# Six small gaps in SBUF: moving a fused convolution-and-MLP kernel's weights and activations apart by 64 to 384 bytes

## The chip, the cores and the metric

The kernel runs on one core of one Trainium2 chip. The metric is the device time of one execution in microseconds (us); lower is better. A core has five engines that run side by side: TensorE (PE, the matrix engine, whose weight loads are shown apart as PEld), VectorE (DVE), ScalarE (ACT), GpSimd (POOL) and SyncE (SP, which here only issues transfers). They work on SBUF, a memory of 128 partitions; an array takes the same byte range in each partition, and the addresses below are byte addresses within a partition. TensorE writes into PSUM.

## The reference

```python
# x, v: (2, 12480, 128)   pos_emb: (12480, 64)
u = x * v
h = (relu(pos_emb @ w1) @ w2) * exp(-0.01 * pos)
y = irfft(rfft(u, 2S) * rfft(h, 2S))[:, :S]        # causal convolution along the sequence, per channel
t = (x * y).reshape(24960, 128)
hid = t @ w_in                                     # (24960, 2048)
g = maximum(0.01 * hid, hid)
out = g @ w_out                                    # (24960, 128)
```

All of it is float32 (the two MLP weights arrive as float64).

## The kernel before

The convolution is a two-stage Fourier transform of 98 x 128 points, done with matmuls against tables. It is computed for sequence 0 first, then for sequence 1 while the MLP of sequence 0 runs. The MLP takes the tokens in 50 tiles of at most 512 columns (46 of 512, two of 352, one of 390, one of 314). Its 2048 hidden channels are taken in 16 slices `f` of 128. Each float32 operand is split into a high and a low part of the type float32r (`zh` and `zl` for the tokens, `w_in_h` and `w_in_l`, and so on), and a product is three matmuls: high by high, high by low, low by high.

So one slice of one tile is six matmuls, and TensorE's stream is this group of six, 800 times over. `m1(k, f)` issues the first three, `m2` the second three for the slice three places earlier (`DEEP = 3`):

```python
nc.tensor.matmul(hp, w_in_h[:, fs], zh, start=True, stop=False)                 # L855
nc.tensor.matmul(hp, w_in_h[:, fs], zl, start=False, stop=False)                # L856
nc.tensor.matmul(hp, w_in_l[:, fs], zh, start=False, stop=True)                 # L857
...
nc.tensor.matmul(ap, w_out_h[:, f, :], rh, start=(f == 0 and at0[k] >= S), stop=False)   # L887
nc.tensor.matmul(ap, w_out_h[:, f, :], rl, start=False, stop=False)             # L888
nc.tensor.matmul(ap, w_out_l[:, f, :], rh, start=False, stop=(f == NF - 1))     # L889
```

The first operand is the one that is loaded into the array (128 columns, PEld, one load for each matmul), the second is streamed through it (the token tile). Between the two threes, ScalarE writes `rh` from `hp` and VectorE writes `rl`. For the 25 tiles of sequence 0, three more matmuls with `wc_h` and `wc_l` (L883 to L885) stand in front of slice 0. Between groups stand the matmuls that bring tokens in and out (`yp` L828, `zp` L836, `op` L911) and those of sequence 1's convolution (`cv` L408 in its first half, `cv` L137, also in threes and mostly of 512 columns, in its second).

The order of all instructions is written out by hand; no scheduler changes it. Arrays are laid out in SBUF in the order in which their pools and tiles are made: the weights stand in the pool `const`, near the start, in the order `ident`, `mb`, `w_in_h`, `w_in_l`, `w_out_h`, `w_out_l`, `wc_h`, `wc_l`; the streamed tiles stand in the pool `sm`, far behind: `zt` (padded to 856 floats, of which 512 are used), `zf`, `zh` and `zl` (three buffers each), `rh` and `rl` (five each). A slice `f` lies 512 bytes behind the slice before it, and a buffer 2048 bytes behind the one before it.

Of the kernel before, what the change touches and what calls it, by code (L numbers as in the profile page):

```python
# [8 lines left out]
F32 = mybir.dt.float32  # L9
# [21 lines left out]
def tile_conv_mlp(ctx, tc, x, v, pos_emb, w1, w2, w_in, w_out, cf, cr, cg, cb, ci, cw, out):  # L31
    nc = tc.nc
    B, S, D = x.shape
# [10 lines left out]
    const = ctx.enter_context(tc.tile_pool(name="const", bufs=1))  # L44
# [9 lines left out]

    ident = const.tile([128, 128], F32, name="ident")
    mb = const.tile([128, 2, 2, 64], F32, name="mb")
    w_in_h = const.tile([128, DFF], F32R, name="w_in_h")
    w_in_l = const.tile([128, DFF], F32R, name="w_in_l")
    w_out_h = const.tile([128, NF, D], F32R, name="w_out_h")
    w_out_l = const.tile([128, NF, D], F32R, name="w_out_l")  # L60
    wc_h = const.tile([128, D], F32R, name="wc_h")
    wc_l = const.tile([128, D], F32R, name="wc_l")
# [91 lines left out]
    def back(dp, parts, c):  # L154

        for s in range(2):
            for j, w in halves(c):
                three(dp[s][:, w], (mi_h[j][:, s], mi_l[j][:, s]), (parts[0][:, s, w], parts[1][:, s, w]))

    def turned(pool, psum, m2, m1):  # L160

        ph = pool.tile([128, 2, 2], F32, tag="ph0", name="ph0", bufs=1)
# [46 lines left out]
    with tc.manual_schedule():  # L209
# [22 lines left out]
        with ExitStack() as st:  # L232
# [81 lines left out]
            for c in range(NC0):  # L314
# [51 lines left out]
                for mm in range(MC):  # L366
                    a = psa.tile([NA, 2, 512], F32, tag="a", name="a", bufs=3)
# [430 lines left out]
        sm = ctx.enter_context(tc.tile_pool(name="sm", bufs=2, reuse_waits="tile"))  # L798
# [16 lines left out]
        def pieces_of(t):  # L815

            for k in range(NTL):
                lo, hi = max(at0[k], t * TOK), min(at0[k + 1], t * TOK + TOK)
                if lo < hi:
                    yield k, lo - at0[k], lo - t * TOK, hi - lo  # L820

        def front(t):

            cp, g, xt = ld.pop(t)
            yp = ps.tile([128, 4, D], F32, tag="io", name="yp")
            for q in range(4):
                for w in range(2):
                    nc.tensor.matmul(yp[64 * w:64 * w + 64, q, :], g[:NA, NA * q + w:NA * q + w + 127:2],  # L828
                                     cp[:, q // 2, w, q % 2, :], start=True, stop=True)
            zt = sm.tile([128, 856], F32, tag="zt", name="zt", bufs=1)[:, :4 * D].rearrange("a (q d) -> a q d", d=D)  # L830
            nc.vector.tensor_tensor(out=zt[:GAP], in0=yp[:GAP], in1=xt[:GAP].rearrange("a p m d -> a (p m) d"),
                                    op=ALU.mult)
            yield
            zp = ps.tile([128, 4, 128], F32, tag="io", name="zp")
            for q in range(4):
                nc.tensor.transpose(zp[:, q, :GAP], zt[:GAP, q, :], ident[:GAP, :GAP])  # L836
            zf = sm.tile([128, TOK], F32, tag="zf", name="zf", bufs=1)
            for w in range(2):
                nc.scalar.copy(zf[:, :2 * NA - 2].rearrange("d (m a) -> d m a", m=2)[:, :, w::2],
                               zp[:, 2:4, 64 * w:64 * w + KH - w])  # L840
            nc.scalar.copy(zf[:, 2 * NA - 2:].rearrange("d (m i w) -> d m w i", m=2, w=2),
                           zp[:, 0:2].rearrange("d m (w i) -> d m w i", w=2)[:, :, :, :KH])
            for k, a, c, n in pieces_of(t):
                if k not in z:
                    z[k] = [sm.tile([128, WIDE], F32R, tag=g, name=g, bufs=ZB) for g in ("zh", "zl")]
                zh, zl = (i[:, a:a + n] for i in z[k])
                nc.scalar.copy(zh, zf[:, c:c + n])  # L847
                (nc.gpsimd if t else nc.vector).tensor_tensor(out=zl, in0=zf[:, c:c + n], in1=zh, op=ALU.subtract)  # L848

        def m1(k, f):  # L850
            w = widths[k]
            zh, zl = (i[:, :w] for i in z[k])
            hp = ps.tile([128, WIDE], F32, tag="mh", name="mh", bufs=3)[:, :w]
            fs = slice(f * 128, f * 128 + 128)
            nc.tensor.matmul(hp, w_in_h[:, fs], zh, start=True, stop=False)  # L855
            nc.tensor.matmul(hp, w_in_h[:, fs], zl, start=False, stop=False)  # L856
            nc.tensor.matmul(hp, w_in_l[:, fs], zh, start=False, stop=True)  # L857
            rh = sm.tile([128, WIDE], F32R, tag="rh", name="rh", bufs=DEEP + 2)[:, :w]
            rl = sm.tile([128, WIDE], F32R, tag="rl", name="rl", bufs=DEEP + 2)[:, :w]
            if at0[k] < S:  # L860
                nc.scalar.activation(out=rh, in_=hp, func=AF.Relu)  # L861
                nc.vector.scalar_tensor_tensor(out=rl, in0=hp, scalar=0.0, in1=rh, op0=ALU.max, op1=ALU.subtract)  # L862
            else:
                tag, pool, bufs = (("s1", s0, 3), ("hd", psc["pool"], 2), ("ct1", psc["pool"], 1),
                                   ("s1", s0, 3), ("hd", psc["pool"], 2))[f % 5]
                r = pool.tile([128, 2048 if tag == "hd" else 1024], F32, tag=tag, name="r", bufs=bufs)[:, :w]
                nc.scalar.activation(out=r, in_=hp, func=AF.Lrelu, alpha=0.01)  # L867
                if f % 2:
                    nc.vector.tensor_copy(rh, r)  # L869
                else:  # L870
                    nc.scalar.copy(rh, r)  # L871
                nc.vector.tensor_tensor(out=rl, in0=r, in1=rh, op=ALU.subtract)  # L872
            return rh, rl
# [71 lines left out]
        def do(what, t):  # L945
            if what == "mult":
                mult_a(t)
            elif what == "conv":
                run(conv)
                load_tile(t)  # L950
                load_tile(t + 1)
            elif what == "load":
                if t not in ld:
                    load_tile(t)
            elif what == "join":
                join_hi(t)
                join_lo(t)
            elif t in fronts:
                next(fronts.pop(t), None)
            else:  # L960
                fronts[t] = front(t)
                next(fronts[t])

        SLOTS = ends[NT] - 14
        done = AHEAD
        frt = front(0)
        join_hi(0)
        join_lo(0)
# [18 lines left out]
        for k in range(NTL):  # L987
            for f in range(NF):
                i = k * NF + f
                pend.append((k, f, m1(k, f)))  # L990
                if len(pend) > DEEP:
                    m2(*pend.pop(0))
                for s_ in steps.get(i, ()):
                    do(*s_)
                if f == DEEP - 1 and k:
                    fin = finish(k - 1)
                if f >= DEEP - 1 and (f - DEEP + 1) % 2 == 0:
                    next(fin, None)
                if i < SLOTS:
                    while done < min(pieces, pace(i)):  # L1000
                        next(conv, None)
                        done += 1
# [71 lines left out]
```

## Time and profile before

| | |
|---|---|
| time, median of 3 runs | 1732.74 us (1730.29 to 1736.19) |
| the profiled execution's own time | 1735.8 us |
| its span from first to last instruction | 1734.0 us |
| TensorE busy | 1650.2 us, 95% of the span |
| VectorE, ScalarE, GpSimd busy | 64%, 57%, 48% |
| mean granted TensorE clock | 0.979 of full speed |
| MLP stage, from about 390 us to the end | 1344 us, TensorE busy 1325.75 us of it, clock 1.00 |

The profiled execution lies 3.1 us above the median, inside the spread of the runs. A matmul's row in the trace gives its start and the length of its record. The records of neighbours overlap, since matmuls are pipelined; what a matmul costs in a dense stretch is the step from its start to the next one's start, not the length of its record.

### The profile page before, as it was taken

To read this page: it belongs to the slowest core of one execution; us is meant where nothing else is said; L and a number is where in the kernel's file an instruction comes from. 1 tells how busy PE (TensorE), PEld (TensorE's weight loads), DVE (VectorE), ACT (ScalarE), POOL (GpSimd) and SP (SyncE) were. 2 spreads that over 40 slices of the span, in tenths; PEclk is the share of its full clock that TensorE was granted. 3 is DMA by queue.
4 is the path that set the end of the run, shared out by engine and by line. 5 is a ranking of instruction groups with operands and counts; after the bars stand their busy time and mean duration, and the time that the engine had idled before them with its cause. 6 is when DMAs were issued, how large, how long until landed. Compare 5 with 4: busy or idle time off the path is not lost.

```text
span 1734.0 us, 27418 instructions
## 1 busy us (share of the span) xinstructions
PE 1650.2 (95%) x9185; PEld 1327.1 (77%) x9185; DVE 1108.7 (64%) x1705; ACT 985.4 (57%) x2005; POOL 833.0 (48%) x858
## 2 busy tenths in 40 slices
PE   6788799889999999999999999999999999999998
PEld 5777455478888887877788777877787878787878
DVE  3586588744554565555555554577777777777775
ACT  1222354434444466666667666566666666666666
POOL 3444122243444277777768675343644454345430
PEclk9889899989999999999999999999999999999999
DMA  8898899964665475556565551222212122111200
GB/s 225 247 263 242 281 322 331 306 201 148 206 182 175 120 200 160 167 154 194 149 175 167 157 150 64 77 67 62 65 43 81 44 70 70 60 53 56 73 18 20
DMA packets 166679, 253.27 MB, mean 146 GB/s; under 512 B 14622, under 2 KB 119346, under 8 KB 163466
## 3 DMA queue, kind: packets, MB, share of 16 engines
q1 hardware_dynamic: 146378, 225.81, 44.8%
q10 hardware_dynamic: 20160, 25.70, 4.3%
q8 instruction: 73, 1.20, 0.3%
q14 instruction: 68, 0.56, 0.1%
HBM read 167.95 MB, written 83.43 MB: 145 GB/s over the span
## 4 chain that ended last, share of the span: by engine, by line
PE 78%; DMA 9%; DVE 5%; issue 3%; SPq 2%; ACT 2%; POOL 1%; ACTq 0%; POOLq 0%; DVEq 0%
PE mh L855 11%; PE mh L857 10%; PE mh L856 10%; PE acc L889 10%; PE acc L887 10%; PE acc L888 10%; PE cv L137 4%; PE yp L828 4%; PE cv L408 3%; DMA ft<-in_cf_dram 2%; DMA xt<-in_x_dram 2%; PE op L911 2%; DMA scr<-o 1%; PE zp L836 1%; DMA scr<-ct 1%
## 5 line engine op out<-in xcount | busy, mean ns | idle before, releaser
L862 DVE SCALAR_TENSOR_TENSOR rl<-mh,rh 128x512 fp32r<-128x512 f32 (+2 forms) x400 | 270.1, 677 | 311.3 <-ACT rh L861 306.9
L872 DVE TENSOR_TENSOR rl<-r,rh 128x512 fp32r<-128x512 f32 (+1 forms) x400 | 329.5, 837 | 113.3 <-ACT rh L871 105.7
L861 ACT ACTIVATE rh<-mh 128x512 fp32r<-128x512 f32 (+2 forms) x400 | 235.2, 590 | 211.7 <-PE mh L857 197.3
L867 ACT ACTIVATE r<-mh 128x512 f32<-128x512 f32 (+1 forms) x400 | 235.7, 590 | 184.8 <-PE mh L857 168.0
L855 PE MATMUL mh<-zh,w_in_h 128*128 128x512 f32 (+3 forms) x800 | 329.8, 412 | 1.9 <-ACT zh L847 1.3
L857 PE MATMUL mh<-zh,w_in_l 128*128 128x512 f32 (+3 forms) x800 | 310.5, 388 | 0.0
L887 PE MATMUL acc<-rh,w_out_h 128*128 128x512 f32 (+3 forms) x800 | 310.3, 388 | 0.0
L856 PE MATMUL mh<-zl,w_in_h 128*128 128x512 f32 (+3 forms) x800 | 310.0, 388 | 0.0
L889 PE MATMUL acc<-rh,w_out_l 128*128 128x512 f32 (+3 forms) x800 | 310.0, 388 | 0.0
L888 PE MATMUL acc<-rl,w_out_h 128*128 128x512 f32 (+3 forms) x800 | 308.3, 385 | 0.0
L848 POOL TENSOR_TENSOR zl<-zf,zh 128x390 fp32r<-128x390 f32 (+24 forms) x110 | 75.7, 702 | 349.7 <-ACT zh L847 349.5
L618 POOL TENSOR_TENSOR cp<-cq,cp 98x256 f32<-98x256 f32 x252 | 212.4, 843 | 19.8
L607 POOL TENSOR_TENSOR cp<-cin 98x256 f32<-98x256 f32 x126 | 104.5, 850 | 162.8 <-PE yp L828 118.7
L855 PEld LDWEIGHTS mh<-zh,w_in_h 128*128 128x128 f32 x800 | 151.1, 189 | 37.0 <-issue 9.9
L857 PEld LDWEIGHTS mh<-zh,w_in_l 128*128 128x128 f32 x800 | 150.8, 189 | 32.1
L888 PEld LDWEIGHTS acc<-rl,w_out_h 128*128 128x128 f32 x800 | 150.4, 188 | 32.1 <-DVE rl L872 0.6
L889 PEld LDWEIGHTS acc<-rh,w_out_l 128*128 128x128 f32 x800 | 150.3, 188 | 31.5
L887 PEld LDWEIGHTS acc<-rh,w_out_h 128*128 128x128 f32 x800 | 150.4, 188 | 30.4
L856 PEld LDWEIGHTS mh<-zl,w_in_h 128*128 128x128 f32 x800 | 151.5, 189 | 24.5 <-POOL zl L848 0.7
L869 DVE CAST rh<-r 128x512 fp32r<-128x512 f32 (+1 forms) x200 | 114.3, 572 | 38.4 <-ACT r L867 35.8
L871 ACT CAST rh<-r 128x512 fp32r<-128x512 f32 (+1 forms) x200 | 122.1, 611 | 6.4
L616 POOL TENSOR_TENSOR cq<-cin 98x256 f32<-98x256 f32 x126 | 113.3, 899 | 1.0 <-DMA cin<-scr 1.0
(154 smaller groups left out, 2359.0 us busy)
## 6 DMA issues: line engine op xcount, KB each, us to landing
cin<-scr SPq DMA_DIRECT2D x318, 98.0 KB
hd<-hspec SPq DMA_DIRECT2D x48, 512.0 KB
scr<-o SPq DMA_DIRECT2D x32, 588.0 KB
bin<-scr SPq DMA_DIRECT2D x23, 768.0 KB
scr1b<-o SPq DMA_DIRECT2D x32, 392.0 KB
hspec<-hs ACTq DMA_DIRECT2D x48, 256.0 KB
scr<-ct ACTq DMA_DIRECT2D x24, 512.0 KB
xm<-in_x_dram SPq DMA_DIRECT2D x128, 96.0 KB
```

The lines of the kernel that those rows point to most:

```text
L618: eng.tensor_tensor(out=cp[:, p, w], in0=cq[:, p], in1=cp[:, p, 1], op=op)
L855: nc.tensor.matmul(hp, w_in_h[:, fs], zh, start=True, stop=False)
L856: nc.tensor.matmul(hp, w_in_h[:, fs], zl, start=False, stop=False)
L857: nc.tensor.matmul(hp, w_in_l[:, fs], zh, start=False, stop=True)
L861: nc.scalar.activation(out=rh, in_=hp, func=AF.Relu)
L862: nc.vector.scalar_tensor_tensor(out=rl, in0=hp, scalar=0.0, in1=rh, op0=ALU.max, op1=ALU.subtract)
L867: nc.scalar.activation(out=r, in_=hp, func=AF.Lrelu, alpha=0.01)
L871: nc.scalar.copy(rh, r)
L872: nc.vector.tensor_tensor(out=rl, in0=r, in1=rh, op=ALU.subtract)
L887: nc.tensor.matmul(ap, w_out_h[:, f, :], rh, start=(f == 0 and at0[k] >= S), stop=False)
L888: nc.tensor.matmul(ap, w_out_h[:, f, :], rl, start=False, stop=False)
L889: nc.tensor.matmul(ap, w_out_l[:, f, :], rh, start=False, stop=(f == NF - 1))
```

## The change

Four tiles that nothing reads are put into `const`, one ahead of each of the MLP's four weight arrays (64, 256, 384 and 64 bytes); `zt`'s padding shrinks by 256 bytes; and a tile of 320 bytes that nothing reads is put ahead of `rh`. The line numbers in the diff are those of the kernel before.

```diff
@@ -54,9 +54,13 @@
     mb = const.tile([128, 2, 2, 64], F32, name="mb")
+    const.tile([128, 16], F32, name="gap_w_in_h")
     w_in_h = const.tile([128, DFF], F32R, name="w_in_h")
+    const.tile([128, 64], F32, name="gap_w_in_l")
     w_in_l = const.tile([128, DFF], F32R, name="w_in_l")
+    const.tile([128, 96], F32, name="gap_w_out_h")
     w_out_h = const.tile([128, NF, D], F32R, name="w_out_h")
+    const.tile([128, 16], F32, name="gap_w_out_l")
     w_out_l = const.tile([128, NF, D], F32R, name="w_out_l")
@@ -827,7 +831,7 @@
-            zt = sm.tile([128, 856], F32, tag="zt", name="zt", bufs=1)[:, :4 * D].rearrange("a (q d) -> a q d", d=D)
+            zt = sm.tile([128, 792], F32, tag="zt", name="zt", bufs=1)[:, :4 * D].rearrange("a (q d) -> a q d", d=D)
@@ -855,6 +859,8 @@
             nc.tensor.matmul(hp, w_in_l[:, fs], zh, start=False, stop=True)
+            if not k and not f:
+                sm.tile([128, 80], F32, tag="gap", name="gap", bufs=1)
             rh = sm.tile([128, WIDE], F32R, tag="rh", name="rh", bufs=DEEP + 2)[:, :w]
```

Every engine has the same instructions, in the same order, with the same waits, before and after; only addresses differ. The program places the arrays so (first buffer of each, bytes):

| array | before | after |
|---|---|---|
| `w_in_h` | 18048 | 18112 |
| `w_in_l` | 26240 | 26560 |
| `w_out_h` | 34432 | 35136 |
| `w_out_l` | 42624 | 43392 |
| `zh` | 149696 | 150208 |
| `zl` | 155840 | 156352 |
| `rh` | 161984 | 162816 |
| `rl` | 172224 | 173056 |

Everything else behind the gaps moves by 512 to 832 bytes, always by a multiple of 64. Since slices lie 512 bytes and buffers 2048 bytes apart, the distance from a streamed tile to a weight slice is the same for all slices and buffers if it is counted modulo 512. While a matmul streams, the weights of the next one are loaded; the distance of a matmul's streamed tile to those weights is:

| matmul (streamed tile), weights loaded meanwhile | before | after |
|---|---|---|
| L855 (`zh`), `w_in_h` for L856 | 64 | 0 |
| L856 (`zl`), `w_in_l` for L857 | 64 | 256 |
| L857 (`zh`), `w_out_h` for L887 | 64 | 384 |
| L887 (`rh`), `w_out_h` for L888 | 64 | 192 |
| L888 (`rl`), `w_out_l` for L889 | 64 | 128 |
| L889 (`rh`), `w_in_h` for the next L855 | 64 | 320 |

The three with `wc_h` and `wc_l` were at 64 too and go to 320. In the second half of sequence 1's convolution (L137) the distance is 160 before and 224 after, and its streamed tiles start 32 bytes off a multiple of 64 in both; all operands of the MLP start on a multiple of 64 in both.

## Rows read from the trace of the kernel before

**Rows 1.** The page's head: span, and busy time (share) and instructions of TensorE.
```profile
span 1734.0 us, 27418 instructions
PE 1650.2 (95%) x9185; PEld 1327.1 (77%) x9185; DVE 1108.7 (64%) x1705; ACT 985.4 (57%) x2005; POOL 833.0 (48%) x858
```

**Rows 2.** The chain that ended last, by engine (page, part 4).
```profile
PE 78%; DMA 9%; DVE 5%; issue 3%; SPq 2%; ACT 2%; POOL 1%; ACTq 0%; POOLq 0%; DVEq 0%
```

**Rows 3.** Busy time by window, the MLP stage; last columns: clock, DMA share, GB/s.
```profile
390.00:1734.00 1344.00, 1325.75 (x6977) 1083.27 (x6975) 851.88 (x1197) 852.00 (x1726) 702.47 (x754) 1.00 0.38 110
```

**Rows 4.** Waits of ScalarE, 390 to 1734 us: total us, times, longest.
```profile
ACT rh L861 <- PE mh L857: 187.7, 203, 3.5
ACT r L867 <- PE mh L857: 168.0, 199, 2.0
```

**Rows 5.** Waits of TensorE's matmuls, 390 to 1734 us, the longest.
```profile
PE op L911 <- ACT zf L841: 11.4, 15, 0.8
```

**Rows 6.** Groups by line and form, whole span: count, busy us, mean record in ns.
```profile
L855 PE MATMUL mh<-zh,w_in_h 128*128 128x512 f32 x736 | 307.0, 417 | 0.6 <-DVE rl L862 0.6
L887 PE MATMUL acc<-rh,w_out_h 128*128 128x512 f32 x736 | 289.6, 393 | 0.0
L889 PE MATMUL acc<-rh,w_out_l 128*128 128x512 f32 x736 | 289.3, 393 | 0.0
L857 PE MATMUL mh<-zh,w_in_l 128*128 128x512 f32 x736 | 289.3, 393 | 0.0
L856 PE MATMUL mh<-zl,w_in_h 128*128 128x512 f32 x736 | 288.6, 392 | 0.0
L888 PE MATMUL acc<-rl,w_out_h 128*128 128x512 f32 x736 | 287.5, 391 | 0.0
```

**Rows 7.** Timeline of TensorE, 1081 to 1096 us: start us, record us, operation.
```profile
1081.13 0.39 PE L857 MATMUL mh<-zh,w_in_l 128*128 128x512 f32 x1
...
1094.87 0.39 PE L857 MATMUL mh<-zh,w_in_l 128*128 128x512 f32 x1
```

**Rows 8.** Groups by line and form, 1081.1 to 1095.7 us.
```profile
L888 PE MATMUL acc<-rl,w_out_h 128*128 128x512 f32 x11 | 4.3, 394 | 0.0
...
L887 PE MATMUL acc<-rh,w_out_h 128*128 128x512 f32 x11 | 4.3, 392 | 0.0
L857 PE MATMUL mh<-zh,w_in_l 128*128 128x512 f32 x11 | 4.3, 388 | 0.0
```

**Rows 9.** Timeline of TensorE, 1213 to 1224 us.
```profile
1213.01 0.40 PE L857 MATMUL mh<-zh,w_in_l 128*128 128x512 f32 x1
...
1214.18 0.40 PE L856 MATMUL mh<-zl,w_in_h 128*128 128x512 f32 x1
...
1222.81 0.40 PE L857 MATMUL mh<-zh,w_in_l 128*128 128x512 f32 x1
```

**Rows 10.** Timeline of the weight loads at 1214 us.
```profile
1214.18 0.19 PEld L857 LDWEIGHTS mh<-zh,w_in_l 128*128 128x128 f32 x1
```

**Rows 11.** Groups by line and form, 1213.0 to 1223.4 us (the other five read 397 too).
```profile
L887 PE MATMUL acc<-rh,w_out_h 128*128 128x512 f32 x8 | 3.2, 397 | 0.0
```

**Rows 12.** Busy time by window, the two stretches of rows 7 and 9.
```profile
1081.10:1095.70 14.60, 14.60 (x65) 11.98 (x64) 6.92 (x10) 6.75 (x12) 4.39 (x6) 1.00 0.42 131
1213.00:1223.40 10.40, 10.40 (x46) 8.43 (x45) 9.32 (x10) 7.65 (x19) 9.18 (x10) 1.00 0.00 1
```

**Rows 13.** Timeline of TensorE, 742 to 744 us.
```profile
742.01 0.39 PE L137 MATMUL cv<-th,mb_h 128*128 128x512 f32 x1
...
743.65 0.39 PE L856 MATMUL mh<-zl,w_in_h 128*128 128x512 f32 x1
```

**Rows 14.** Groups by line and form, 600 to 1100 us (six of 396 to 400).
```profile
L137 PE MATMUL cv<-th,mb_l 128*128 128x512 f32 x48 | 19.1, 398 | 0.0
```

## The prediction

> **What bounds the kernel now.** I read the page's head first, then the chain, then the MLP stage alone. TensorE is busy for 95% of the span [rows 1], and the chain that ended last runs over it for 78% [rows 2]. From 390 us on TensorE is busy 1325.75 of 1344 us at full clock [rows 3]. The other engines wait for it there: ScalarE alone stands idle 187.7 and 168.0 us for the result of the first three matmuls [rows 4], while the longest wait of TensorE's matmuls for somebody else sums to 11.4 us [rows 5]. So in this stage a nanosecond added to every matmul is a nanosecond added to the kernel, and nothing else sets the pace.
>
> The stage is 4,800 MLP matmuls (800 groups of six) and 75 with `wc_h` and `wc_l`, 4,875 in all; 4,416 of the 4,800 are 512 columns wide (six rows of 736 [rows 6]). What matters is the step from one start to the next. It is not one number. From 1081.13 to 1094.87 us there are 60 steps in 13.74 us, 229.0 ns each [rows 7]. From 1213.01 to 1222.81 us there are 42 steps of the same kind in 9.80 us, 233.3 ns each [rows 9]. The records show two rhythms behind these means. In the first stretch they go 392, 394, 388 and begin again, whatever the line (the other three lines of the six read 388, 392 and 394 as well) [rows 8]; in the second all are 397 [rows 11]. The second stretch is the slower one although next to no transfer is on its way in it (DMA share 0.00, against 0.42 in the first) [rows 12], so transfers are not what slows it; and both have the full clock.
>
> How much of the stage runs in which rhythm follows from the mean records. The first rhythm's mean is (392 + 394 + 388) / 3 = 391.3, the second's 397. Over the whole stage the five lines that do not follow a change of work average 392.4 [rows 6] (L855 often comes right behind the token matmuls, and its 417 holds that change). (392.4 - 391.3) / (397 - 391.3) = 0.19, so about a fifth lies in the second rhythm, and the mean step is 229.0 + 0.19 x 4.3 = 229.8 ns. That is the figure that the change can move.
>
> **The change, part by part.** It adds no instruction, removes none, moves none and changes no wait, so there is nothing to add up on any queue. The tiles that fill the gaps are never written or read. Only addresses differ, and the only place where that can matter for the time is the stage's own pace: everything else is off the path (ScalarE's idle time above), and all shifts are multiples of 64 bytes.
>
> The weights of L857 begin to load at 1214.18 us [rows 10], the same 10 ns in which L856 begins to stream [rows 9]. So TensorE reads a streamed tile and a weight array at once, and the one relation between them that the change touches is their distance: 64 bytes (modulo 512) in all six cases before, six other values after, none of them 64.
>
> Does the distance matter? The trace before has one other distance at the same width and the same type: the convolution's matmuls, at 160. From the first of them at 742.01 us to the matmul at 743.65 us there are seven steps in 1.64 us, 234.3 ns each [rows 13], and their records over the whole run average 396 to 400, against 391 to 393 for the MLP's [rows 14, 6]. They differ from the MLP's in two things, the distance and a start 32 bytes off a multiple of 64, so the row leans towards "it matters" without settling it. A record is some 163 ns longer than its step in both rhythms (391.3 against 229.0, 397 against 233.3), so 388, the shortest of the first rhythm, stands for a step of about 226.
>
> [...]
>
> No row shows the price of the six new distances, so it is bounded from both sides. Below: all matmuls at the shortest step that a row stands for, 226, which is 3.8 ns x 4,875 = 18.5 us less. Above: all at the 234.3 of the convolution's, 4.5 ns x 4,875 = 22 us more; the longest of those records, 400, stands for 237 and would be 35 us more. Between them I take the mean of the three steps that the trace shows over several matmuls, (229.0 + 233.3 + 234.3) / 3 = 232.2. The reason: the rhythm of 229.0 belongs to a stream in which all six distances are equal and it comes back every three matmuls, whatever their operands; six different distances break that sameness, and then no row favours one step over another. 232.2 - 229.8 = 2.4 ns, times 4,875, is 11.7 us more. The profiled execution's 1735.8 would become 1747.5; it stands 3.1 us above the median of its runs, so the forecast is 1732.7 + 11.7, about 1744 to 1745.
>
> **The rivals.** *Distance is nothing to TensorE.* Then the two rhythms come from something else, for instance from the moment at which a dense stretch begins, and the convolution's 234.3 comes from its 32 bytes. For it speaks that both rhythms occur at one and the same distance [rows 7, 9]. Against it speaks only the convolution's step [rows 13]. It gives the time before, 1733, plus or minus 5 for the share of the second rhythm: were that share 0 the stage would lose 0.8 ns x 4,875 = 4 us, were it doubled it would gain as much. [...]
>
> *The new distances are better than 64.* The mechanism: if the streamed reads and the weight load get in each other's way for part of each load, and 64 is a distance at which they do, then matmuls at a distance where they do not take 226 or less, and even the six as a mixture come out below 229.0. For it speaks that even the fastest rhythm has records that differ by 6 ns for like work [rows 8], so some waiting is in it that a better place could remove. Against it speaks that the only other distance in the trace is slower. If all six are at 226 the time is 1732.7 - 18.5 = 1714; with half of that gain, 1723. It decides the sign from a mean step of 229.8 - 5.2 / 4.875 = 228.7 ns downwards.
>
> *The worse end.* All six behave like the convolution's products or like the second rhythm: 233.3 to 234.3 throughout, 17 to 22 us more, 1750 to 1755. This is my forecast's own case with a worse price, and is counted with it.
>
> **How the numbers follow.** A measurement of this kernel tells about 0.3%, 5.2 us, from no change. The distances matter and the mixture is worse: 0.47, with 1738 to 1757 as its own range and 1745 as its value. No effect to speak of: 0.22, 1728 to 1738. Better: 0.31, 1712 to 1727. The range that leaves out no more than 2 in 10 reaches from 1714, the better case's full price, to 1757, the worse case's end.
>
> **What would show it.** In the profile after, every instruction count must be as before, and the stage must again be dense (TensorE busy over 98% of it, full clock). If my step is right, the six lines' mean records go apart: each line gets its own, since each has its own distance, their mean lies near 395, and the pattern that repeats every three matmuls is gone. If the distance is nothing, 392, 394, 388 and 397 come back, on all lines alike. If the better case holds, some lines read 388 or less and none over 394. The convolution's matmuls (from 160 to 224) should change their 396 to 400 only if distance counts. Wrong altogether would be a change outside the MLP stage: before 390 us, where transfers set the pace, I expect less than 2 us.

## The result

The changed kernel takes 1743.93 us (median of 6 runs, 1740.72 to 1746.93), the kernel before 1733.99 us in the 6 runs beside it: a ratio of 1.0058, with a 95% interval of 1.0040 to 1.0077. It is slower by about 10 us. Its profiled execution has a span of 1745.1 us, 11.1 us more than that of before [rows 1].

The head of its page: the count of instructions is the same, and TensorE is busy 10.4 us longer, while VectorE, ScalarE and GpSimd do the same work in the same time.

```profile
span 1745.1 us, 27418 instructions
PE 1660.6 (95%) x9185; PEld 1329.4 (76%) x9185; DVE 1107.4 (63%) x1705; ACT 985.2 (56%) x2005; POOL 831.1 (48%) x858
```

Busy time by window, the MLP stage, which now ends at 1745 us. It is 11 us longer, as dense as before and at full clock [rows 3]:

```profile
390.00:1745.00 1355.00, 1337.06 (x6975) 1085.98 (x6973) 851.87 (x1197) 851.88 (x1725) 701.06 (x754) 1.00 0.38 109
```

Waits in that stage: ScalarE's for TensorE grew by 2.6 and 3.1 us [rows 4], and the longest wait of TensorE's matmuls is what it was [rows 5]. Nobody new holds TensorE up.

```profile
ACT rh L867 <- PE mh L861: 190.3, 200, 3.5
ACT r L873 <- PE mh L861: 171.1, 199, 2.0
```
```profile
PE op L917 <- ACT zf L845: 11.4, 15, 0.8
```

The first matmul of the MLP starts at 365.0 us, against 366.3 before, and the last L859 at 1737.0 us, against 1725.8 for its counterpart. What stands ahead of the MLP lost nothing; the MLP stage took all of it.

Groups by line and form, count, busy us and mean record in ns (L859 to L861 are L855 to L857 of before, L893 to L895 are L887 to L889). The five lines that follow no change of work read 391 to 393 before [rows 6]. Now they have gone apart, two at 393 and three at 396, 394.8 on average:

```profile
L859 PE MATMUL mh<-zh,w_in_h 128*128 128x512 f32 x736 | 308.1, 419 | 0.6 <-DVE rl L868 0.6
L860 PE MATMUL mh<-zl,w_in_h 128*128 128x512 f32 x736 | 291.6, 396 | 0.0
L895 PE MATMUL acc<-rh,w_out_l 128*128 128x512 f32 x736 | 291.3, 396 | 0.0
L894 PE MATMUL acc<-rl,w_out_h 128*128 128x512 f32 x736 | 291.3, 396 | 0.0
L861 PE MATMUL mh<-zh,w_in_l 128*128 128x512 f32 x736 | 289.5, 393 | 0.0
L893 PE MATMUL acc<-rh,w_out_h 128*128 128x512 f32 x736 | 289.4, 393 | 0.0
```

The timeline of TensorE (start us, record us) in the longest stretch that holds only the six matmuls. It is the same piece of the program as the stretch of [rows 7], and again the rows stand 60 steps apart:

```profile
1085.60 0.40 PE L861 MATMUL mh<-zh,w_in_l 128*128 128x512 f32 x1
...
1099.54 0.39 PE L861 MATMUL mh<-zh,w_in_l 128*128 128x512 f32 x1
```

13.94 us over 60 steps is 232.3 ns, where it was 229.0 [rows 7]. All start times together say the same. The steps of under 250 ns from one 512-column matmul of the six lines to the next, which hold no other work, average 229.9 ns before (3,957 steps) and 232.3 ns after (3,961), and they add up to 909.6 and 920.2 us: 10.6 of the 11.1 us that the span grew.

### The profile page after: what moved, and what is told of

Its sections match the earlier page's. It is cut to its first block, busy times and chain, and to the rows that moved or that the text cites. A ratio compares the mean times of both kernels' runs of the same rounds, so it can differ in the third digit from the quotient of the medians.

```text
span 1745.1 us, 27418 instructions
## 1 busy us (share of the span) xinstructions
PE 1660.6 (95%) x9185; PEld 1329.4 (76%) x9185; DVE 1107.4 (63%) x1705; ACT 985.2 (56%) x2005; POOL 831.1 (48%) x858
## 4 chain that ended last, share of the span: by engine, by line
PE 79%; DMA 9%; DVE 4%; issue 3%; ACT 2%; SPq 1%; POOL 1%; ACTq 0%; POOLq 0%; DVEq 0%
PE mh L859 11%; PE mh L860 10%; PE mh L861 10%; PE acc L894 10%; PE acc L895 10%; PE acc L893 10%; PE cv L141 4%; PE yp L832 4%; PE cv L412 3%; DMA xt<-in_x_dram 2%; PE op L917 2%; DMA hspec<-hs 1%; DMA scr<-ct 1%; PE zp L840 1%; DMA vt<-in_v_dram 1%
## 5 line engine op out<-in xcount | busy, mean ns | idle before, releaser
L859 PE MATMUL mh<-zh,w_in_h 128*128 128x512 f32 (+3 forms) x800 | 330.9, 414 | 2.0 <-ACT zh L851 1.4
L894 PE MATMUL acc<-rl,w_out_h 128*128 128x512 f32 (+3 forms) x800 | 312.6, 391 | 0.0
L895 PE MATMUL acc<-rh,w_out_l 128*128 128x512 f32 (+3 forms) x800 | 312.4, 390 | 0.0
L861 PE MATMUL mh<-zh,w_in_l 128*128 128x512 f32 (+3 forms) x800 | 311.2, 389 | 0.0
L893 PE MATMUL acc<-rh,w_out_h 128*128 128x512 f32 (+3 forms) x800 | 310.7, 388 | 0.0
L859 PEld LDWEIGHTS mh<-zh,w_in_h 128*128 128x128 f32 x800 | 152.8, 191 | 38.6 <-issue 10.0
L893 PEld LDWEIGHTS acc<-rh,w_out_h 128*128 128x128 f32 x800 | 150.8, 189 | 33.9
L861 PEld LDWEIGHTS mh<-zh,w_in_l 128*128 128x128 f32 x800 | 150.6, 188 | 33.7
L894 PEld LDWEIGHTS acc<-rl,w_out_h 128*128 128x128 f32 x800 | 150.8, 189 | 32.3 <-DVE rl L878 0.6
L895 PEld LDWEIGHTS acc<-rh,w_out_l 128*128 128x128 f32 x800 | 150.7, 188 | 31.8
```

## The experiments

Every kernel below has the instructions of before; only gaps and paddings differ. In the texts on record L855 to L857 and L887 to L889 mean the six lines by their numbers in the kernel before. "The stretch" is that of 60 steps shown above, which every kernel has.

**All distances kept, all places moved.**

```diff
+    const.tile([128, 80], F32, name="gap_w_in_h")
     w_in_h = const.tile([128, DFF], F32R, name="w_in_h")
```

> One gap of 320 bytes ahead of the first weight array moves all weights and all streamed tiles together: the six distances stay 64, every address changes. Theory (the distance sets the step): 1731 to 1737 us, a mean step of 230 ns and again the records 392, 394, 388 that repeat every three matmuls. Rival (the place itself counts, not the distance): a mean step elsewhere, 232 or more, 1741 us or more.

Measured: 1732.71 us, ratio 1.0000 (0.9989 to 1.0012), as the theory had it. The 60 steps take 13.73 us, 228.8 ns each, against 229.0 before; the rows round a start to 10 ns, so such a mean is good to 0.2 ns. The places of the MLP's arrays, moved together by 320 bytes, count for nothing as long as their distances stay (L858 is L857 of before):

```profile
1077.40 0.40 PE L858 MATMUL mh<-zh,w_in_l 128*128 128x512 f32 x1
...
1091.13 0.39 PE L858 MATMUL mh<-zh,w_in_l 128*128 128x512 f32 x1
```

**All six distances 0, 256 or 160.** One number changes, `zt`'s padding (840, 904 and 880 floats in place of 856):

```diff
-            zt = sm.tile([128, 856], F32, tag="zt", name="zt", bufs=1)
+            zt = sm.tile([128, 840], F32, tag="zt", name="zt", bufs=1)
```

> Padding of zt smaller by 64 bytes: all six distances 0 instead of 64. The changed kernel has 0 only behind L859, whose step there is the longest of its six (mean 235.1 ns). Theory (each distance has its own price): a mean step near 235, 1734 + 4875 x 5 ns, about 1758 us. Rival (what counts is that the six are equal, so that a rhythm can settle): 229 to 231 ns, 1730 to 1737 us.

Measured: 1726.28 us, ratio 0.9960 (0.9946 to 0.9974): faster than both kernels. The prices by distance that I had read off the changed kernel's six lines were wrong: 0 stands there behind the line with the longest step (L859, 235.1 ns), and a stream with nothing but 0 is the quickest so far (227.0 ns), quicker than the rival's 229 to 231 ns too. Its timeline, 60 steps of 227.0 ns:

```profile
1079.05 0.39 PE L857 MATMUL mh<-zh,w_in_l 128*128 128x512 f32 x1
...
1092.67 0.39 PE L857 MATMUL mh<-zh,w_in_l 128*128 128x512 f32 x1
```

> Padding of zt larger by 192 bytes: all six distances 256. In the changed kernel the matmul at 256 (L860) has a mean step of 233.0 ns. Theory (each distance has its own price): a mean step near 233, about 1748 us. Rival (equal distances let a rhythm settle): 229 to 231 ns, 1730 to 1737 us.

Measured: 1725.39 us, ratio 0.9955 (0.9939 to 0.9971), 13.63 us for the 60 steps, and in the groups of six the same steps as at 0 (227, 226, 227, 227, 226, 227, over and over once they have settled); 227.2 and 227.0 differ by rounding alone:

```profile
1074.88 0.39 PE L857 MATMUL mh<-zh,w_in_l 128*128 128x512 f32 x1
...
1088.51 0.39 PE L857 MATMUL mh<-zh,w_in_l 128*128 128x512 f32 x1
```

> Padding of zt larger by 96 bytes: all six distances 160 and all streamed tiles of the MLP start 32 bytes off a multiple of 64, as those of the convolution did before. Theory (distance): the convolution's step of 234.3 ns, 1734 + 4875 x 4.2 ns, about 1754 us; records that repeat every seven matmuls. Rival (the convolution's step came from something else in it): 230 ns, 1734 us.

Measured: 1747.32 us, ratio 1.0080 (1.0066 to 1.0094), the slowest here, though its interval overlaps that of the changed kernel. 14.05 us for the 60 steps are 234.2 ns, where the convolution's matmuls at 160 gave 234.3 [rows 13], and the steps repeat every seven (231, 238, 237, 231, 234, 235, 234); the time that was expected, 1754 us, was 7 us too long. So equality alone does not make a stream quick either: here all six share 160, and the step is 234.2 ns.

```profile
1082.60 0.39 PE L857 MATMUL mh<-zh,w_in_l 128*128 128x512 f32 x1
...
1096.65 0.39 PE L857 MATMUL mh<-zh,w_in_l 128*128 128x512 f32 x1
```

**How far apart two equal distances may be.** `zt` at 872 and 888 floats:

> All six distances 128 (padding of zt larger by 64 bytes). If the pattern repeats every 128 bytes, as 0 and 256 gave one and the same step, this is 0 again: a steady step of 226.7 ns, a mean of 228.7, 1726 us. If it repeats only every 256, 128 is a new distance and the step may be anything from 226 to 238 ns (1715 to 1770 us).

Measured: 1742.84 us, ratio 1.0054 (1.0035 to 1.0073), 13.94 us for the 60 steps, 232.3 ns. It is no 0 again (227.0 ns), while 256 was (227.2): a pattern that repeats every 128 bytes is out, and one that repeats every 256 fits the three:

```profile
1082.52 0.39 PE L857 MATMUL mh<-zh,w_in_l 128*128 128x512 f32 x1
...
1096.46 0.40 PE L857 MATMUL mh<-zh,w_in_l 128*128 128x512 f32 x1
```

> All six distances 192. If the pattern repeats every 128 bytes, this is 64 again: the rhythms of 229.0 and 233.3 ns, 1731 to 1737 us. If only every 256, it is a new distance, and its time is open.

Measured: 1745.71 us, ratio 1.0072 (1.0051 to 1.0093), 233.3 ns in the stretch. It is not 64 again, although 233.3 is also the step of 64's slower rhythm [rows 9]: of the groups of six that hold no other work (under 1410 ns from the first start to that behind the last) none takes 1376 ns or less here (477 groups), where 344 of 472 do so in the kernel before.

**Two values in one stream.** From the kernel with all six at 0, a gap ahead of `rh` of 64 bytes (16 floats), and in the second kernel of 256 (64 floats):

```diff
+            if not k and not f:
+                sm.tile([128, 16], F32, tag="gap", name="gap", bufs=1)
             rh = sm.tile([128, WIDE], F32R, tag="rh", name="rh", bufs=DEEP + 2)[:, :w]
```

> Three of the six distances are 0 (L855 to L857), three are 64 (L887 to L889): two values, each of which is quick when all six have it (1726 and 1733 us). Theory (unequal distances break the rhythm): a mean step of 231 ns or more, 1738 us or more. Rival (each distance has its own price, whatever the neighbours have): the mean of the two, 229.2 ns, 1729 to 1731 us.

Measured: 1745.13 us, ratio 1.0069 (1.0051 to 1.0088). This is the run that decides whether being unequal costs by itself. Three matmuls at a distance that gives 227.0 ns when all have it, and three at one that gives 229.0, make a stream of 13.97 us / 60 = 232.8 ns, worse than either:

```profile
1087.32 0.39 PE L857 MATMUL mh<-zh,w_in_l 128*128 128x512 f32 x1
...
1101.29 0.39 PE L857 MATMUL mh<-zh,w_in_l 128*128 128x512 f32 x1
```

> Three distances 0, three 256. Equal distances gave the same step at 0 and at 256, so if only the distance modulo 256 counts these six are equal: 226.7 ns steady, 1726 us, like all six at 0. If being unequal in itself costs, 1738 us or more.

Measured: 1726.63 us, ratio 0.9964 (0.9950 to 0.9978), 13.63 us for the 60 steps. That is 227.2 ns: 0 and 256 side by side act as equal distances:

```profile
1076.26 0.39 PE L857 MATMUL mh<-zh,w_in_l 128*128 128x512 f32 x1
...
1089.89 0.39 PE L857 MATMUL mh<-zh,w_in_l 128*128 128x512 f32 x1
```

**Which weights count.** Again from all six at 0. In the first kernel `zl` alone moves (64 bytes ahead of it, 448 ahead of `rh`), in the second `w_in_l` alone, the other way (448 bytes ahead of it, 64 ahead of `w_out_h`):

```diff
-                    z[k] = [sm.tile([128, WIDE], F32R, tag=g, name=g, bufs=ZB) for g in ("zh", "zl")]
+                    z[k] = [sm.tile([128, WIDE], F32R, tag="zh", name="zh", bufs=ZB)]
+                    if not k:
+                        sm.tile([128, 16], F32, tag="gapz", name="gapz", bufs=1)
+                    z[k].append(sm.tile([128, WIDE], F32R, tag="zl", name="zl", bufs=ZB))
...
+            if not k and not f:
+                sm.tile([128, 112], F32, tag="gap", name="gap", bufs=1)
```
```diff
+    const.tile([128, 112], F32, name="gap_w_in_l")
     w_in_l = const.tile([128, DFF], F32R, name="w_in_l")
+    const.tile([128, 16], F32, name="gap_w_out_h")
     w_out_h = const.tile([128, NF, D], F32R, name="w_out_h")
```

> From the kernel with all six at 0, zl alone is moved by 64 bytes (64 ahead of zl, 448 ahead of rh). Only L856 streams zl: its distance to the weights that load meanwhile (w_in_l) and to its own (w_in_h) both go to 64. One unequal distance of six: the rhythm of 226.7 ns should go, and the mean step lie between 229 and 233 ns (1729 to 1748 us).

> From the kernel with all six at 0, w_in_l alone is moved by 64 bytes the other way (448 ahead of it, 64 ahead of w_out_h). If the weights that load meanwhile count, L856 is the one at 64 and the six lines' mean steps are those of the run in which zl was moved, line by line, within 0.3 ns. If a matmul's own weights count, L857 is the one at 64 instead, and the pattern of the six means is the other run's, one line later.

Measured: 1738.56 us, ratio 1.0029 (1.0018 to 1.0041), and 1737.66 us, ratio 1.0014 (1.0004 to 1.0025). Against all six at 0, by the ratios (1.0029 and 1.0014 against 0.9960), one unequal distance costs 9 to 12 us. The first kernel's time lies in the range that was expected of it. The six lines' mean steps, in the order of the program, are 229.2, 232.4, 236.5, 228.4, 230.4, 232.6 with `zl` moved and 228.5, 229.0, 233.6, 230.2, 231.6, 230.1 with `w_in_l` moved (steps over 250 ns left out). They are neither the same nor the same one line later, so neither of the two cases of the second expectation came. In both the longest step is that of L857, the line behind L856, which leans towards the weights that load meanwhile; the test does not settle it. A kernel in which `zl` and `w_in_l` move together was not run: it would leave all six distances to the weights that load meanwhile equal, and change those of L856 and L857 to their own weights.

**Between the two best.** `zt` at 848 floats:

> All six distances 32, between the two best so far (mean steps 228.7 at 0, 229.8 at 64; 233.2 at 192). If the price is a smooth curve of the distance with its low between 0 and 64: 226 to 229 ns, 1715 to 1728 us. If a start that is not a multiple of 64 costs by itself, 233 ns, 1748 us.

Measured: 1742.98 us, ratio 1.0053 (1.0039 to 1.0067), 233.3 ns in the stretch. No smooth curve with a low between 0 and 64. Whether 32 is a bad distance or a start 32 bytes off a multiple of 64 is a bad start this run can't tell, since it has both, as the one at 160 has.

**The convolution's matmuls too.** All six at 0, and 160 bytes ahead of the tiles that L137 streams:

```diff
         psc["pool"] = ctx.enter_context(tc.tile_pool(name="sb1", bufs=2, reuse_waits="tile"))
+        psc["pool"].tile([128, 40], F32, tag="gaps", name="gaps", bufs=1)
```

> All six distances 0, and 160 bytes ahead of the convolution's tiles, so that its 306 matmuls (L137) lie at 0 modulo 256 too. Theory (equal distances keep the rhythm, through the convolution's matmuls as well): their step goes from about 233 to 227, 306 x 6 ns = 1.8 us, and the MLP's matmuls behind them save some more: 1722 to 1725 us. Rival (only the MLP's own six count): 1726 us.

Measured: 1724.01 us, ratio 0.9946 (0.9933 to 0.9959), the lowest time of all. The convolution's records are shorter, 389 to 396 ns, where the kernel before has 396 to 400 [rows 14] and the kernel with all six at 0 has 396 to 402; by groups, two of the six (L137 has kept its number):

```profile
L137 PE MATMUL cv<-th,mb_l 128*128 128x512 f32 x48 | 18.7, 390 | 0.0
L137 PE MATMUL cv<-tl,mb_h 128*128 128x512 f32 x48 | 18.7, 389 | 0.0
```

The step from 1726.28 to 1724.01 us itself is not settled by the times: the two ratios' intervals overlap. That the place of its tiles counts for the convolution's matmuls too is shown by their own steps; distance and start are not told apart, since at 0 modulo 256 the tiles also start on a multiple of 64. In the kernel with all six at 0 the smaller padding had taken them from 160 to 96, and from one of them to the next they average 234.9 ns (119 steps); here, at 0, 227.2. In the kernel with all six at 160 it was they that came to 0 modulo 256: their steps fell to 229.4, from 233.4 before, while the MLP's rose.

The uniform streams side by side (step in the stretch; the one at 64 is the kernel before):

| all six at | 0 | 32 | 64 | 128 | 160 | 192 | 256 |
|---|---|---|---|---|---|---|---|
| step, ns | 227.0 | 233.3 | 229.0 | 232.3 | 234.2 | 233.3 | 227.2 |
| ratio to before | 0.9960 | 1.0053 | 1 | 1.0054 | 1.0080 | 1.0072 | 0.9955 |

## Why the prediction was right

**What bounds the kernel** held: the stage is as dense as before, and the time it lost lies in the steps between its matmuls (10.6 of 11.1 us).

**The size** held. The forecast step was 232.2 ns, 2.4 more than before, worth 11.7 us; measured are 232.3 over all steps that hold no other work, 2.4 more than before, and about 10 us. The sum's 4,875 counts too many, since only some 3,960 steps hold no other work. That 232.2 came out so exactly is in part luck: it is a mean of three steps, taken because no row gave a price. And the range was wide: all kernels measured here, from 1724 to 1747 us, lie in it.

What the profile after was to show came in part: a mean record near 395 (394.8), nothing lost ahead of the MLP (365.0 against 366.3 us), and convolution records that moved only a little (394 to 400). But the lines did not get a record each. Five lines show two values, and L861 and L894, both at 128 modulo 256, differ (393 and 396).

**The reason** held in one half. "Six different distances break that sameness" is what two runs show by themselves: three at 0 and three at 64 give 232.8 ns where the mean of the two uniform streams would be 228.0, and a single one of six at 64 costs 9 to 12 us. For the changed kernel the prices of its distances, taken modulo 256 from the table (0 twice, 128 twice, 64 and 192), average (2 x 227.0 + 2 x 232.3 + 229.0 + 233.3) / 6 = 230.2 ns. So of the 3.3 ns that the stretch lost, an estimated 1.2 belong to the distances themselves and 2.1 to their being unequal; were it the distance to a matmul's own weights that counts (0 three times, 192 twice, 128), the mean would be 230.0, and the shares 1.0 and 2.3. "Then no row favours one step over another" was the weak half: the mean of the three steps that the trace showed came out right, but the uniform streams lay anywhere from 227.0 to 234.2. Nor does inequality end all rhythm: in the changed kernel 300 of 475 undisturbed groups of six take 1393 or 1394 ns, a rhythm of six matmuls in place of three, only a slower one.

**The rivals.** "Distance is nothing to TensorE" fell: seven uniform streams differ by up to 7.2 ns a step (227.0 to 234.2), and the five whose tiles start on a multiple of 64 by 6.3 (227.0 to 233.3), while the streamed tiles and the weights can all move together with no effect (rigid shift, ratio 1.0000). "The new distances are better than 64" was half true: 0 and 256, which two of the six got, are better, but the runs show it only for streams in which all six have 0 or 256 (227.0 to 227.2 ns); three at 0 beside three at 64 gave 232.8. Its price was sized too high: 226 ns for every matmul was to bring 18.5 us; all six at 0 run at 227.0 ns in undisturbed stretches and brought 0.40%, 7 us, since behind each insertion of other work the rhythm has to settle again: the first six steps there average 230.6 ns, the next six 227.3, those behind them 226.7. "The worse end" was sized too high as well, but not for that reason: at 160 the step is 234.2 ns, like the convolution's, priced at 22 us and measured at 0.80%, 14 us. There the first six steps read 234.0, like the rest; the steps without other work take 18.0 us more than before, and the steps of over 250 ns and the convolution's together 4.1 us less.

A rival that the prediction leaves out is the work of the other engines on SBUF: in the slower of its two stretches VectorE and GpSimd are busy about 90% of the time [rows 12]. The traces speak against it. With all six at 0 the quarter of the groups of six in which VectorE is busiest steps at 227.2 ns, that in which it is least busy at 228.6, and with all six at 192 every quarter reads 233.1 to 233.3. That it has a say in which of its two rhythms a stream at 64 falls into is not excluded: in the kernel before GpSimd is busy for 76% of the time of the slow groups and for 54% of that of the fast ones.

**What stays open.** By what the distance acts, which no run shows, whether a matmul's own weights or those loaded meanwhile count (the two runs made for it fit neither), and why 32 is slow between 0 and 64. Why a stream at 64 has two rhythms, 229.0 and 233.3, is not settled either; the distances alone do not fix their shares, since 68 of 472 groups take 1396 ns or more before, and 20 of 471 with all places moved and the distances kept. That two distances 256 apart cost the same was measured in the MLP for 0 and 256 only; 128 and 64 stand for 384 and 320 in the mean above on the assumption that it holds there too.

## What to carry to other kernels

Where TensorE is the bound and one float32r matmul follows the other, look at the step from start to start and at records that repeat in a pattern: here, with all starts on a multiple of 64, the step of a uniform stream was 227.0 to 233.3 ns, by the byte distance between the streamed tile and the weights. Make that distance the same for all matmuls of the stream, modulo 256, and try 0 first; it costs a padding, and was worth 0.4 to 0.5% here. Do not judge a distance by a line of a mixed stream: the line with the longest step here (235.1 ns) had the distance that is quickest when all share it (227.0).

## What was not expected

Where it was measured, the distance counts modulo 256 bytes, though slices lie 512 and buffers 2048 bytes apart: 0 and 256 give steps of 227.0 and 227.2 ns, and mixed in one stream 227.2 (13.63 us over 60 steps), while 128 gives 232.3. The convolution's matmuls stand at 96 in the kernel with all six at 0 and at 352, which is 96 modulo 256, in the one with all six at 256, and step at 234.9 in both. And two quick distances in one stream (227.0 and 229.0) make a slow one (232.8).
